# A new order for the first group of an mLSTM and SwiGLU kernel

## The chip, the cores and the metric

The kernel runs on one core of a Trainium2 chip. The metric is the time of one execution on the device in microseconds (us). Five engines work side by side, each through its own instructions in a fixed order: TensorE (PE, matrix products), VectorE (DVE), ScalarE (ACT), GpSimd (POOL) and SyncE (SP, which here only issues DMAs). An engine that waits holds up everything that stands behind the waiting instruction.

## The reference

First comes an mLSTM cell with q, k, v and an output gate of shape (4, 8, 768, 40): batch, heads, steps, width. The cell's rows, heads side by side, are then the 3072 x 320 input of a SwiGLU block.

```python
for t in range(S):                       # for every batch and head
    m_new  = max(f_gate[t] + m, i_gate[t])
    f_stab = exp(f_gate[t] + m - m_new);  i_stab = exp(i_gate[t] - m_new)
    C = f_stab * C + i_stab * outer(v[t], k[t])
    n = f_stab * n + i_stab * k[t]
    y[t] = sigmoid(o_gate[t]) * (C @ q[t]) / max(abs(n @ q[t]), 1)
g = x @ w_gate                           # x: y as (3072, 320); w_gate, w_val: (320, 1536)
out = (g * sigmoid(g) * (x @ w_val)) @ w_out      # w_out: (1536, 320)
```

## The kernel before

**Groups.** The 768 steps are cut into six groups of 128 steps (`L`), and a group of all four batches gives 512 rows for the SwiGLU block. The recurrence is computed in chunks: inside a chunk as masked and weighted scores, across chunks through a state `C`. The 32 pairs of batch and head are worked on in two halves, `P` = 0 and 1. Group 0 has its own code (the functions named `first_...`), since it has no state before it; the other groups go through `turn`, `scores`, `weigh`, `add`, `next_state`, `attend`, `gather`, `gate`, `divide` and `seam`.

**Group 0**, in front of everything: `first_mask`, `first_inputs` and `first_maxima` build the exponents of the weights in PSUM, `first_exp` exponentiates them into `h_sb` (which is free until the hidden blocks need it), `first_turn` transposes k and q on PE and copies them out, `first_scores` multiplies k and q on PE, and DVE multiplies the weights by it (line 480). `first_own(u)` multiplies the weights by v for batch u, `first_x(u)` divides (lines 492 to 495), `first_gate(P)` multiplies by the output gate, whose sigmoid `sig(P)` is taken on ACT, `first_seam(P, engs)` transposes the result into `xT`, with the engines of its three copies given as letters (A is ACT, V is DVE), and `first_state(P, eng)` makes the state for the next group. `late_sums` and `late_maxima` are the running sums and maxima of the gates for groups 1 to 5. `burn(n)` issues n matmuls on a tile of zeros whose result nobody reads.

**Hidden blocks.** `hidden(g, m)` makes block m of twelve of the hidden layer of group g: ten fp32 matmuls (line 593), a SiLU on ACT (598) and a product on DVE (599). Then `project` or `project_all` multiplies by `w_out` (609, 616). In group 0, further work is hung between the hidden blocks by hand in a table `slots`: after block m, the calls of `slots[m]` are issued.

**Weights.** They arrive as fp32 in pieces (`piece_load`), by SP's queue. `convert(j)` rounds block j in three steps: `scale` on ACT (lines 184 and 186, from `raw` to `top` and `low`), `join` on DVE (194, 195, to `both`) and `rounded` (202) on POOL, or on DVE where V is given: block 0 and, by `on_vector`, blocks 9, 10 and 11. `top`, `low` and `both` have one buffer each, so block j+1 follows block j. In the loop over group 0, `convert(m + 2)` is issued behind the matmuls of block m and ahead of its SiLU. Pieces 0 and 1 hold one block each, pieces 2 to 6 two blocks each (piece 6: blocks 10 and 11), pieces 7 to 9 hold `w_out`. The tile `raw` has two buffers, so the load of piece 4 waits until `scale(0)` has read piece 0, and so on.

**Weights of the scores in group 1.** `late_maxima` stores the maxima to memory (`M_dram`, line 285), `weights_load` reads them back spread over partitions into `w_sb` (404), `weights_sub` subtracts on DVE (408), `weights_mask` masks on POOL (413, two instructions for each P), `weights_exp` exponentiates on ACT (417), and `weigh_values` multiplies v by the last column on POOL (320).

**What sets the order.** The kernel is written under a manual schedule: on each engine the instructions stand in the order in which the functions are called. PSUM is eight banks in two rotations of four: "cell" (transposes, scores, adds, burns) and "gen" (first_own, hidden blocks, projections). A bank is taken again only when the tile four before it in the same rotation has been read.

Of the kernel before, what the change touches and what calls it, by code (L numbers as in the profile page):

```python
# [24 lines left out]
def kernel(  # L25
# [47 lines left out]
    def flat(t):  # L73
        return t.rearrange("p c t -> p (c t)")

    def bank(name, tag="cell"):
        return psum.tile([128, 512], F32, name=name, tag=tag)

    def half(i):
        return slice(i * SUB, (i + 1) * SUB)  # L80

    def heads(P):
        return slice(P * UH, (P + 1) * UH)

    k_sb = const.tile([128, BH, DP], F32)
    q_sb = const.tile([128, BH, DP], F32)
# [5 lines left out]
    qT = const.tile([128, PP, L], F32)  # L92
# [22 lines left out]
    def copy(eng, dst, src):  # L115
        if eng is nc.scalar:
            nc.scalar.copy(dst, src)
        else:
            eng.tensor_copy(dst, src)
# [59 lines left out]
    def scale(j):  # L179
        if j in blocks:  # L180
            lo, hi, dst = blocks[j]
            a, d = hi.shape[1], hi.shape[2]
            top = conv.tile([128, NKC * 128], F32, name="top", bufs=1).rearrange("p (a d) -> p a d", a=a)
            nc.scalar.mul(top, hi.bitcast(F32), 2.0 ** -112)  # L184
            low = conv.tile([128, NKC * 128], I32, name="low", bufs=1).rearrange("p (a d) -> p a d", a=a)
            nc.scalar.mul(low, lo, 2.0 ** -29)
            blocks[j] = (low, top.bitcast(U32), dst)

    def join(j):
        if j in blocks:  # L190
            lo, top, dst = blocks[j]
            a = dst.shape[1]
            both = conv.tile([128, NKC * 128], U32, name="both", bufs=1).rearrange("p (a d) -> p a d", a=a)
            nc.vector.tensor_scalar(both, top, scalar1=3, scalar2=None, op0=ALU.logical_shift_left)  # L194
            nc.vector.scalar_tensor_tensor(both, in0=top, scalar=0x80000000, in1=both, op0=ALU.bitwise_and,  # L195
                                           op1=ALU.bitwise_or)
            blocks[j] = (lo, both, dst)

    def rounded(j, eng=None):
        if j in blocks:  # L200
            lo, both, dst = blocks.pop(j)
            (eng or nc.gpsimd).tensor_tensor(dst.bitcast(I32), both.bitcast(I32), lo, op=ALU.add)  # L202

    def convert(j, eng=None):
        scale(j)
        join(j)
        rounded(j, eng)
# [64 lines left out]
    def late_sums():  # L272
        nc.vector.tensor_tensor_scan(flat(f_sb), flat(keep1), flat(f_sb), 0.0, op0=ALU.mult, op1=ALU.add)
        nc.gpsimd.memset(step1, 0.0)
        nc.vector.tensor_sub(i_sb, i_sb, f_sb)
        nc.vector.tensor_copy(step1[:, 0:1, 0:1], f0[0:BH, end].unsqueeze(1))
        nc.vector.tensor_copy(step1[:, 1:, 0:1], f_sb[:, 0:NL - 1, last])
# [57 lines left out]
    def state(s):  # L335
        return C_ring[s % 3]
# [82 lines left out]
    def sig(P):  # L419
        nc.scalar.activation(o_sb[:, heads(P)], o_sb[:, heads(P)], AF.Sigmoid)  # L420


    def burn(n):
        t = bank("burn")
        for _ in range(n):
            nc.tensor.matmul(t, lhsT=junk[:, 0:128], rhs=junk, start=True, stop=True)
# [4 lines left out]
    A, V, G = nc.scalar, nc.vector, nc.gpsimd  # L431
# [29 lines left out]
    def first_turn(P, src, dst, engs):  # L461
        for b in range(2):
            tp = bank("tp_kq").rearrange("p (a t) -> p a t", t=L)
            for a in range(UA // 2):
                h = P * UH + b * H + 2 * a
                nc.tensor.transpose(tp[:, a, :], src[:, h:h + 2, :].rearrange("p h d -> p (h d)"), ident)
            a = P * UA + b * UA // 2
            copy(engs[b], dst[:, a:a + UA // 2, :], tp)

    def first_scores(P):  # L470
        for b in range(2):
            sp = [bank("sp").rearrange("p (a t) -> p a t", t=L) for _ in range(2)]
            a0 = P * UA + b * UA // 2
            for a in range(UA // 2):
                for two in range(2):
                    nc.tensor.matmul(sp[two][:, a, :], lhsT=kT[half(two), a0 + a, :], rhs=qT[half(two), a0 + a, :],
                                     start=True, stop=True)
            W = W0[:, 2 * a0:2 * a0 + H].rearrange("p (a two) t -> p two a t", two=2)
            for two in range(2):
                nc.vector.tensor_tensor(W[:, two], sp[two], W[:, two], op=ALU.mult)  # L480
# [3 lines left out]
    def first_own(u):  # L484
        first_y[u] = bank("first_y", "gen")[:, 0:H * D1].rearrange("p (h d) -> p h d", d=D1)
        for h in range(H):
            nc.tensor.matmul(first_y[u][:, h, :], lhsT=W0[:, u * H + h, :], rhs=v_sb[:, u * H + h, :], start=True, stop=True)

    def first_x(u):
        y = first_y.pop(u)  # L490
        den = work.tile([128, UH, 1], F32, name="den")[:, 0:H]
        nc.vector.tensor_scalar(den, y[:, :, D:], scalar1=1.0, scalar2=None, op0=ALU.max)
        nc.vector.scalar_tensor_tensor(den, in0=y[:, :, D:], scalar=-1.0, in1=den, op0=ALU.mult, op1=ALU.max)
        nc.vector.reciprocal(den, den)
        nc.vector.tensor_tensor(x_sb[:, u, 0:DM].rearrange("p (h d) -> p h d", d=D), y[:, :, 0:D],
                                den.to_broadcast([128, H, D]), op=ALU.mult)

    def first_gate(P):
        for u in (2 * P, 2 * P + 1):
            x = x_sb[:, u, 0:DM].rearrange("p (h d) -> p h d", d=D)  # L500
            nc.vector.tensor_tensor(x, x, o_sb[:, u * H:(u + 1) * H], op=ALU.mult)
        nc.gpsimd.tensor_copy(x_sb[:, 2 * P:2 * P + 2, DM:], x_sb[:, 2 * P:2 * P + 2, 0:HP])

    def first_state(P, eng):
        ps = small("add")
        for a in range(UA):
            for two in range(2):
                h = P * UH + 2 * a + two
                nc.tensor.matmul(ps[half(two), a, :], lhsT=k_sb[:, h, :], rhs=vw_sb[:, h, :], start=True, stop=True)
        copy(eng, state(2)[:, P * UA:(P + 1) * UA], ps)  # L510

    def first_seam(P, engs):
        for c, eng in zip(range(0, NKC, 2), engs):
            cs = range(c, min(c + 2, NKC))
            tp = bank("tp_x")[:, 0:len(cs) * 2 * L].rearrange("p (c u s) -> p c u s", u=2, s=L)
            for w in cs:
                for b in range(2):
                    nc.tensor.transpose(tp[:, w - c, b, :], x_sb[:, 2 * P + b, ds(PAIRS[w][0] * HP, 2 * HP)], ident)
            copy(eng, xT(0)[:, c:c + len(cs), 2 * P * L:(2 * P + 2) * L].rearrange("p c (u s) -> p c u s", u=2), tp)
# [10 lines left out]
    first_exp(1)  # L530
    first_values(0)
    first_scores(0)
    late_sums()
    first_own(0)
    first_turn(1, k_sb, kT, (A, A))
    first_own(1)
    first_turn(1, q_sb, qT, (A, V))
    sig(0)
    first_values(1)
    first_x(0)  # L540
    first_x(1)
    first_scores(1)
    first_own(2)
    first_own(3)
    first_x(2)
    first_gate(0)
    first_x(3)
    sig(1)
    first_seam(0, (A, A, A))
    first_gate(1)  # L550
    first_state(0, A)
    first_seam(1, (V, A, V))
    first_state(1, A)
    burn(6)
    convert(0, V)
    convert(1)


    pair = early.tile([BH, PP], F32)
# [94 lines left out]
    def load_all(dst, a, n):  # L654
        for P in range(2):
            load(dst, a, n, P)

    run = lambda f, *a: (lambda: f(*a))
# [3 lines left out]
    slots = {  # L662
        0: [run(load_all, k_sb, k, 1), run(load_all, q_sb, q, 1), run(piece_load, 5), run(late_maxima)],
        1: [run(decay_rows)],
        2: [run(late_turns), run(weights_load, 1)],
        3: [run(decay)],
        4: [run(piece_load, 6), run(load_all, v_sb, v, 1)],
        5: [run(turn, 0, (A, A), (A, V))],
        6: [run(turn, 1, (A, A), (A, V)), run(piece_load, 7)],
        7: [run(weights_sub, 1, 0), run(weights_mask, 0)],  # L670
        8: [run(weights_sub, 1, 1), run(weights_mask, 1), run(weights_exp, 0), run(weights_exp, 1),
            run(weigh_values, G, 0), run(weigh_values, G, 1), run(piece_load, 8)],
        9: [run(do_scores), run(do_weigh, 0), run(load_all, o_sb, o_gate, 1)],
        10: [run(do_weigh, 1), run(do_add), run(do_state, 2, 0), run(do_state, 2, 1), run(piece_load, 9)],
        11: [run(do_attend, 1, 0), run(do_gather, 1, 0, False)],
# [1 line left out]
    piece_load(4)  # L677
    for m in range(NFC):
        hidden(0, m, [run(convert, m + 2, V if m + 2 in on_vector else None)])
        for f in slots[m]:  # L680
            f()
    after = {
        0: [run(do_attend, 1, 1), run(convert, 14), run(sig, 0), run(sig, 1), run(do_gate, 0)],
# [21 lines left out]
    for g in range(1, NG):  # L705
        n, f = g + 1, g + 2
        slots = {m: [] for m in range(NFC)}
# [63 lines left out]
```

## Time and profile before

| what | value |
|---|---|
| runs | 584.78, 584.83, 587.49 us; median 584.83 |
| profiled execution | 583.13 us, of which the span of instructions is 581.3 us |
| mean granted TensorE clock | 0.994 |
| busy in the span | PE 567.3 us, DVE 209.2, ACT 150.9, POOL 99.6 |
| first matmul of hidden block 0 | at 37.62 us |
| first matmul of group 1 (its block 0) | at 138.03 us |

The profile is of one execution. Its lines of the timeline give start in us, duration in us, engine, source line, operation, output and inputs with shapes, and the number of instructions merged into one line; the bracket gives the idle time of the engine before it and who ended it. PEclk is the TensorE clock granted, 1.00 being full speed. SPq lines are DMA issues; their duration is how long SP took to issue, not to move the data.

### The profile page before, as it was taken

What the parts mean: (1) busy time and instruction counts of PE and PEld (TensorE: products, weight loads), DVE (VectorE), ACT (ScalarE), POOL (GpSimd) and SP (SyncE); (2) the same over time, 40 slices, a digit from 0 to 9 for tenths busy, and PEclk for the clock granted to TensorE, in tenths of its full rate; (3) what the DMA queues carried; (4) which work ended last, traced back from release to release, by engine and by line L of the source; (5) the groups of instructions that cost most, each with busy time, mean ns of one, the idle gap of its engine ahead of it and who ended that gap; (6) DMA issues with size and microseconds to landing.
All of it is one profiled execution on the core that took longest, in us unless ns stands there. A gap on an engine that the chain in (4) does not pass through costs nothing.

```text
span 581.3 us, 12164 instructions
## 1 busy us (share of the span) xinstructions
PE 567.3 (98%) x5404; PEld 329.7 (57%) x5405; DVE 209.2 (36%) x379; ACT 150.9 (26%) x236; POOL 99.6 (17%) x101
## 2 busy tenths in 40 slices
PE   8889988999999999999999999999999999999997
PEld 4854534666555576555566555567555557544475
DVE  5846475880335520334620233640223640011100
ACT  4356555434401115210114311024301110011100
POOL 2122325445001132002132001232001110000000
PEclk9989999999999999999999999999999999999999
DMA  9999896395223711304340304360000000000000
GB/s 124 185 209 154 178 201 153 119 159 106 41 29 43 126 28 36 45 2 70 76 78 24 58 1 47 64 113 23 12 2 2 2 1 24 23 1 0 1 23 23
DMA packets 129915, 37.85 MB, mean 65 GB/s; under 512 B 120424, under 2 KB 125032, under 8 KB 129864
## 3 DMA queue, kind: packets, MB, share of 16 engines
q1 hardware_dynamic: 129636, 36.85, 36.7%
q8 instruction: 42, 0.69, 0.5%
q10 hardware_dynamic: 228, 0.23, 0.2%
q14 instruction: 9, 0.07, 0.0%
HBM read 33.06 MB, written 4.01 MB: 64 GB/s over the span
## 4 chain that ended last, share of the span: by engine, by line
PE 81%; ACT 2%; DVE 1%; DMA 0%; issue 0%; ACTq 0%; DVEq 0%
PE gv_ps L593 45%; PE o_ps L609 22%; PE o_ps L616 4%; PE inter L350 2%; PE intra L355 2%; PE add L331 2%; PE sp L310 1%; PE tp_kq L295 1%; PE tp_x L396 1%; ACT w_sb L417 0%; DMA out_dram<-z_sb 0%; ACT o_sb L420 0%; ACT L598 0%; ACT L420 0%; ACT L417 0%
## 5 line engine op out<-in xcount | busy, mean ns | idle before, releaser
L593 PE MATMUL gv_ps<-xT,wgv_sb 64*128 64x512 f32 x1440 | 323.4, 597 | 5.1 <-DVE wgv_sb L202 5.1
L593 PEld LDWEIGHTS gv_ps<-xT,wgv_sb 64*128 64x128 f32 x1440 | 138.2, 188 | 161.9 <-issue 152.3
L599 DVE TENSOR_TENSOR h_sb<-sg,gv_ps 128x512 f32<-128x512 f32 x72 | 49.4, 687 | 304.2 <-ACT sg L598 287.3
L609 PE MATMUL o_ps<-wo_sb,h_sb 128*128 128x320 f32 x480 | 130.5, 433 | 0.0
L598 ACT ACTIVATE sg<-gv_ps 128x512 f32<-128x512 f32 x72 | 43.0, 598 | 269.2 <-PE gv_ps L593 269.2
L609 PEld LDWEIGHTS o_ps<-wo_sb,h_sb 128*128 128x128 f32 x480 | 90.8, 190 | 38.2 <-issue 0.8
L340 POOL TENSOR_TENSOR C<-C,dec 128x328 f32<-128x328 f32 x20 | 14.5, 737 | 165.0 <-DVE C L342 165.0
L603 ACT COPY z_sb<-o_ps 128x320 f32<-128x320 f32 x24 | 10.2, 426 | 114.4 <-PE o_ps L609 103.0
L413 POOL TENSOR_SCALAR_AFFINE_SELECT w_sb<-w_sb 64x1024 f32<-64x1024 f32 x20 | 26.3, 1314 | 29.6 <-DVE w_sb L408 28.7
L616 PE MATMUL o_ps<-wo_sb,h_sb 128*128 128x320 f32 x96 | 26.9, 437 | 0.0
L376 POOL TENSOR_TENSOR o_sb<-o_sb,y_sb 128x640 f32<-128x640 f32 x10 | 14.2, 1429 | 48.4 <-DVE y_sb L367 48.4
L616 PEld LDWEIGHTS o_ps<-wo_sb,h_sb 128*128 128x128 f32 x96 | 17.9, 190 | 7.2
L367 DVE TENSOR_TENSOR y_sb<-y_sb,intra 64x328 f32<-64x328 f32 x40 | 19.7, 493 | 0.9
L320 POOL TENSOR_TENSOR vw_sb<-v_sb,w_sb 128x656 f32<-128x656 f32 x10 | 12.8, 1306 | 29.4 <-issue 29.3
L202 POOL TENSOR_TENSOR wgv_sb<-both,low 128x640 int32<-128x640 int32 x8 | 12.3, 1540 | 30.3 <-DVE both L195 30.3
L195 DVE SCALAR_TENSOR_TENSOR both<-top,both 128x640 uint32<-128x640 uint32 x18 | 15.7, 870 | 0.6
L194 DVE TENSOR_SCALAR both<-top 128x640 uint32<-128x640 uint32 x18 | 10.2, 565 | 12.9 <-ACT top L184 10.4
L350 PEld LDWEIGHTS inter<-C,qT 64*64 64x64 f32 x640 | 10.2, 134 | 7.3 <-issue 6.1
L202 POOL TENSOR_TENSOR wo_sb<-both,low 128x640 int32<-128x640 int32 x6 | 10.2, 1704 | 18.3 <-DVE both L195 12.9
L184 ACT ACTIVATE top<-raw 128x640 f32<-128x640 f32 x14 | 11.1, 795 | 8.2 <-DVE both L195 5.8
L408 DVE TENSOR_TENSOR w_sb<-g_T,w_sb 128x1024 f32<-128x1024 f32 x10 | 13.2, 1350 | 0.0
L342 DVE TENSOR_TENSOR C<-C,add 128x328 f32<-128x328 f32 x20 | 9.8, 492 | 8.7 <-POOL C L340 8.7
(120 smaller groups left out, 379.2 us busy)
## 6 DMA issues: line engine op xcount, KB each, us to landing
w_sb<-M_dram SPq DMA_DIRECT2D x10, 512.0 KB, 6.7
k_sb<-in_k_dram SPq DMA_DIRECT2D x12, 320.0 KB, 7.0
q_sb<-in_q_dram SPq DMA_DIRECT2D x12, 320.0 KB, 4.1
v_sb<-in_v_dram SPq DMA_DIRECT2D x12, 320.0 KB, 5.5
o_sb<-in_o_gate_dram SPq DMA_DIRECT2D x12, 320.0 KB, 6.8
raw<-in_moe_w_out_dram SPq DMA_DIRECT2D x3, 1280.0 KB, 7.3
out_dram<-z_sb SPq DMA_DIRECT2D x24, 160.0 KB, 1.8
raw<-in_moe_w_gate_dram SPq DMA_DIRECT2D x3, 640.0 KB, 9.3
```

Source lines behind the costliest of these rows:

```text
L195: nc.vector.scalar_tensor_tensor(both, in0=top, scalar=0x80000000, in1=both, op0=ALU.bitwise_and, op1=ALU.bitwise_or)
L202: (eng or nc.gpsimd).tensor_tensor(dst.bitcast(I32), both.bitcast(I32), lo, op=ALU.add)
L340: nc.gpsimd.tensor_tensor(state(s + 1)[:, a], state(s)[:, a], dec[:, s - 2, a].unsqueeze(2).to_broadcast([128, UA, D1]), op=ALU.mult)
L350: nc.tensor.matmul(inter[two][half(i), a, :], lhsT=qT[half(two), P * UA + a, half(i)], rhs=state(2 * n + i)[half(two), P * UA + a, :], sta ...
L367: nc.vector.tensor_tensor(t, t, intra[i][half(c)], op=ALU.add)
L376: eng.tensor_tensor(o, o, y[:, :, 0:D], op=ALU.mult)
L413: nc.gpsimd.affine_select(w, w, compare_op=ALU.is_ge, fill=NEG, base=0, pattern=[[0, UH], [1, SUB]], channel_multiplier=-1)
L593: nc.tensor.matmul(ps[i], lhsT=wgv_sb[half(i), PAIRS[kc][i], ts(m, 128)], rhs=x[half(i), kc, :], start=(kc == 0), stop=(kc == NKC - 1))
L598: nc.scalar.activation(sg, ps[0], AF.Silu)
L599: nc.vector.tensor_tensor(hid(g, m), sg, ps[1], op=ALU.mult)
L609: nc.tensor.matmul(p, lhsT=hid(g, m)[:, ts(u, L)], rhs=wo_sb[:, m, :], start=(m == 0), stop=(m == NFC - 1))
L616: nc.tensor.matmul(ps[u], lhsT=hid(g, m)[:, ts(u, L)], rhs=wo_sb[:, m, :], start=(m == 0), stop=(m == NFC - 1))
```

## The change

The calls of group 0 are put in a new order, which is a new order on every engine. The transposes of q for P = 1 go ahead of `first_own(1)`. `first_x(0)` follows the transposes of k. Both sigmoids come together. `burn(6)` at the end becomes `burn(3)`, `burn(5)` and `burn(4)` at three places. `first_gate` of P = 0 goes ahead of `first_x(2)`. The third copy of each `first_seam` goes to DVE and the first two to ACT. `scale(0)` and `join(0)` are issued between the two seams and `rounded(0)` behind the second. Both `first_state` follow both seams. `late_sums` moves from the middle to behind `convert(1)`.

In the table for group 0, slot 5 becomes empty: the two `turn` calls move from slots 5 and 6 to 6 and 7, both `weights_sub` and both `weights_mask` stand together in slot 7, and slot 8 keeps the exponentials, `weigh_values` and the load of piece 8. SP's DMAs stay in the same order. Nothing is computed differently.

```diff
     first_scores(0)
-    late_sums()
     first_own(0)
     first_turn(1, k_sb, kT, (A, A))
+    first_x(0)
+    first_turn(1, q_sb, qT, (A, V))
     first_own(1)
-    first_turn(1, q_sb, qT, (A, V))
-    sig(0)
     first_values(1)
-    first_x(0)
     first_x(1)
     first_scores(1)
+    sig(0)
+    sig(1)
+    burn(3)
     first_own(2)
     first_own(3)
+    first_gate(0)
     first_x(2)
-    first_gate(0)
+    first_seam(0, (A, A, V))
+    burn(5)
     first_x(3)
-    sig(1)
-    first_seam(0, (A, A, A))
     first_gate(1)
+    scale(0)
+    join(0)
+    first_seam(1, (A, A, V))
+    rounded(0, V)
     first_state(0, A)
-    first_seam(1, (V, A, V))
     first_state(1, A)
-    burn(6)
-    convert(0, V)
+    burn(4)
     convert(1)
+    late_sums()
...
-        5: [run(turn, 0, (A, A), (A, V))],
-        6: [run(turn, 1, (A, A), (A, V)), run(piece_load, 7)],
-        7: [run(weights_sub, 1, 0), run(weights_mask, 0)],
-        8: [run(weights_sub, 1, 1), run(weights_mask, 1), run(weights_exp, 0), run(weights_exp, 1),
-            run(weigh_values, G, 0), run(weigh_values, G, 1), run(piece_load, 8)],
+        6: [run(turn, 0, (A, A), (A, V)), run(piece_load, 7)],
+        7: [run(turn, 1, (A, A), (A, V)), run(weights_sub, 1, 0), run(weights_sub, 1, 1), run(weights_mask, 0),
+            run(weights_mask, 1)],
+        8: [run(weights_exp, 0), run(weights_exp, 1), run(weigh_values, G, 0), run(weigh_values, G, 1),
+            run(piece_load, 8)],
```

More of the change, by code (lines that the diff above doesn't have):

```diff
@@ L679 @@
         hidden(0, m, [run(convert, m + 2, V if m + 2 in on_vector else None)])
-        for f in slots[m]:
+        for f in slots.get(m, ()):
             f()
```

## The prediction

> **What bounds the kernel now.** The page gives TensorE (PE) 567.3 us of a span of 581.3. A gain is therefore either idle PE time, or PE time at a low clock, ahead of 100 us; behind that the matmuls stand end to end. The page's DMA row (40 slices of 14.5 us) and the waits of PE:
>
> ```profile
> DMA  9999896395223711304340304360000000000000
> PE gv_ps L593 <- DVE wgv_sb L202: 5.1, 4, 2.2
> ```
>
> The loads fill every slice up to 72 us, and PE's longest waits are for weights (`wgv_sb`) that VectorE (DVE) has rounded. PE's timeline shows where; from here on h0 to h11 are the twelve hidden blocks of the first group:
>
> ```profile
> 78.66 4.56 PE L593 MATMUL gv_ps<-xT,wgv_sb 64*128 64x512 f32 x20 [0.19 <-DVE wgv_sb L202]
> 84.61 4.56 PE L593 MATMUL gv_ps<-xT,wgv_sb 64*128 64x512 f32 x18 [1.39 <-DVE wgv_sb L202]
> 89.09 2.10 PE L310 MATMUL sp<-qT,kT 64*64 64x64 f32 x128
> 91.12 1.12 PE L593 MATMUL gv_ps<-xT,wgv_sb 64*128 64x512 f32 x2
> 93.60 4.55 PE L593 MATMUL gv_ps<-xT,wgv_sb 64*128 64x512 f32 x18 [1.35 <-DVE wgv_sb L202]
> ```
>
> These are h8, h9, the scores of group 1, and h10, whose first matmul runs alone before the rest waits. DVE shows what they wait for:
>
> ```profile
> 80.68 1.22 DVE L194 TENSOR_SCALAR both<-top 128x640 uint32<-128x640 uint32 x1 [0.35 <-ACT top L184]
> 81.93 1.63 DVE L195 SCALAR_TENSOR_TENSOR both<-top,both 128x640 uint32<-128x640 uint32 x1
> 83.73 0.83 DVE L202 CUSTOM_DVE_ANT_0 wgv_sb<-both,low 128x1280 uint16<-128x1280 uint16 x1 [0.17 <-DVE both L195]
> 92.72 0.83 DVE L202 CUSTOM_DVE_ANT_0 wgv_sb<-both,low 128x1280 uint16<-128x1280 uint16 x1 [0.17 <-DVE both L195]
> ```
>
> Blocks 9, 10 and 11 are rounded on DVE. Block 10's rounding ends at 84.56 and lets **h9** go at 84.61; block 11's ends at 93.55 and lets **h10** go: the DVE rounding is taken for a write to the whole tile, so each block waits for the rounding of the next. What held those two back stands on ScalarE (ACT) and GpSimd (POOL):
>
> ```profile
> 79.86 0.79 ACT L184 ACTIVATE top<-raw 128x640 f32<-128x640 f32 x1 [1.61 <-DMA raw<-in_moe_w_val_dram]
> 88.72 1.06 ACT L417 ACTIVATE w_sb<-w_sb 128x1024 f32<-128x1024 f32 x1 [3.34 <-POOL w_sb L413]
> 89.68 0.80 ACT L184 ACTIVATE top<-raw 128x640 f32<-128x640 f32 x1
> 80.41 2.49 POOL L413 TENSOR_SCALAR_AFFINE_SELECT w_sb<-w_sb 64x1024 f32<-64x1024 f32 x2 [7.57 <-DVE w_sb L408]
> 86.36 2.33 POOL L413 TENSOR_SCALAR_AFFINE_SELECT w_sb<-w_sb 64x1024 f32<-64x1024 f32 x2 [3.46 <-DVE w_sb L408]
> ```
>
> Block 10 starts when piece 6 has landed (79.86). Its join (L194, L195) then runs beside the mask of pair half 0 and takes 1.22 and 1.63, against 0.49 and 0.82 elsewhere. Block 11 (89.68) stands on ACT behind exp(1), which waits for mask(1). Why piece 6 lands at 79.86 is on SP's queue and in the list of DMA issues:
>
> ```profile
> 56.56 0.55 SPq L285 DMA_DIRECT2D M_dram<-M_sb  x1
> 64.92 2.12 SPq L404 DMA_DIRECT2D w_sb<-M_dram  x2
> 67.13 2.70 SPq L159 DMA_DIRECT2D raw<-in_moe_w_gate_dram  x1
> 69.88 1.28 SPq L159 DMA_DIRECT2D raw<-in_moe_w_val_dram  x1
> M_dram<-M_sb SPq DMA_DIRECT2D x1, 80.0 KB, 8.4
> ```
>
> 80 KB take 8.4 us, since they queue behind the loads issued before; SP stands still until 64.92 for them, and piece 6 is issued after. So **79.86 is a date of the DMA queue**, not of any engine. Last, two stretches of the windows view (us, then PE, PEld, DVE, ACT, POOL busy, PEclk, DMA share, GB/s):
>
> ```profile
> 27.70:31.10 3.40, 3.40 (x30) 2.90 (x29) 2.06 (x7) 1.45 (x3) 0.59 (x2) 0.51 1.09 211
> 38.00:41.30 3.30, 3.30 (x10) 1.39 (x8) 1.51 (x4) 1.74 (x3) 1.54 (x1) 0.50 1.07 215
> ```
>
> PE ran at half clock for 3.4 us twice, both in the part that the change rewrites.
>
> [...] two stretches of 3.4 us, the second after 2.17 us of idle PE (35.45 to 37.62). The first followed no long gap, only 128x41 matmuls[...]. [...]
>
> **The change part by part.**
>
> *Front.* In the old order DVE did late_sums (2.5 us) and both first_x of P=0 (4 instructions, 1.1 us each) before the last score products, which began at 22.98. In the new one the transposes of q (P=1) go ahead of first_own(1): that load has landed by about 17.8 (issued at 10.25; the v load behind it landed at 20.0; 2.2 us each), so first_own(1) ends at about 20.4 and the scores start at 20.4 as before (20.50). first_x(1) then ends at 21.6, and the products run 21.6 to 24.1: 1.4 earlier. PE: scores to 22.4, burn(3) 0.7 (0.25 each: 1.47 for six in the row of 33.98), first_own(2) and (3) 3.5, to 26.6 (before 27.85). first_seam(0) at full clock takes 1.3 (2.49 before), burn(5) 1.2. DVE: gate(0) 24.1 to 25.0, x(2), a seam copy at 28.0, x(3) and gate(1) to 30.3. first_seam(1) 30.0 to 31.7, both states 2.1, burn(4) 1.0: h0 at about **34.7** (37.62 before). Weights: scale(0) runs behind the first two seam copies on ACT (28.4 to 29.9; piece 0 was issued at 20.9 and takes 5.3), join(0) to 31.6, rounding to 33.1: hidden. With the 1.7 us of half clock at 38.0 to 41.3 gone (if the 12 burns keep the clock up; 6 before), h0 ends 4.6 earlier. late_sums now sits on DVE behind join(1), about 36.5 to 39, ahead of block 2's join and h0's product; POOL's memset likewise ahead of rounding 2. The maxima are ready at about 43, and their store stands in SP's queue until 56.56 anyway: free.
>
> *DMAs.* SP's order is the same. Piece 4 can be issued at 30 instead of 35.92, k of group 1 at 33.8 instead of 37.27, but [...] the dates 56.56, 64.92 and 79.86 stay. Value: 0.
>
> *Slots 5 to 8.* turn moves from slots 5 and 6 to 6 and 7. turn(1), 0.98 us of transposes, now covers the rounding of block 9 between h7 and h8 (a bubble of 1.1 before). h8 then ends at about 34.7 + 9x4.35 (h4 and h5: 8.69) + 3.2 (small transposes 0.73, decay 0.47, turns 0.98 and 0.99) = 77.1 instead of 83.0. Both subs (1.22 each) run on DVE from about 74.2 to 76.6, the four masks (1.17 each) on POOL to about 80.1, just clear of join(10) at 80.5.
>
> *From piece 6 on.* join(10) 0.49+0.82 instead of 1.22+1.63: h9 at 83.0, **1.6 earlier**. The lead of 5.8 that h8 had is waited away there. ACT: scale(10) to 81.15, silu(8), table 1.28, both exps to 85.1, scale(11) to 86.5; join(11) to 88.0 even beside weigh_values on POOL; rounding to 88.9. PE: h9 4.5, scores 2.0: h10 at 89.4, no wait. Before it had lost 93.60 - 91.12 = **2.5** there. Sum 4.1. Later work keeps its own spacing.
>
> *Against it.* Between h8's end (the lone first matmul of h9 included: about 78.1) and 83.0 PE idles 4.9 us, far more than the 2.17 that cost the clock before. [...] I take **1.5**.
>
> Net -2.6 against the profiled execution's 583.13: 580.5. The median of the runs, 584.83, is 1.7 above that execution, as much as one whole 3.41 us stretch at half clock costs. If it is one in the waits before h10, it goes with them (580.5); if it is anything else it stays (582.2). The trace can't tell; I take between: **581.4**.
>
> **Rivals.**
> 1. *The clock holds through the wait*: -4.1, so 579.0 to 580.7. Against: 2.17 us were enough. Chance 0.12.
> 2. *The DMA date moves up*, because pieces 4 and k are issued 3.5 to 6 earlier; dips in the rate of the 160-byte loads (45 to 60 us: 157 GB/s against 210) leave room for 1 to 2. About 579.5. Against: the queue never ran dry. Chance 0.15.
> 3. *The masks still meet join(10)*: the margin is 0.4 us. Up to 1.5 of the 1.6 goes: -1.0, so 582 to 584. Chance 0.18.
> 4. *Slower*: late_sums is late, the maxima miss their place in SP's queue, and SP holds w_sb and piece 6 behind them. One for one from 56.6; slower by over 0.5% from about 62. For it: five instructions were moved 20 us back. Against: a margin of 13 us. About 588. Chance 0.10.
> The main case has 0.45.
>
> **How the numbers follow.** 0.5% is 2.9 us, about what a measurement of this kernel can tell from no change. The main case spans 580 to 583.5 with somewhat over half below 581.9; with rivals 1 and 2: faster 0.56. The rest of it and rival 3: same 0.34. Rival 4: slower 0.10. The range 579.0 to 584.0 leaves out rival 4 and the tails of 1 to 3.
>
> **What would show it.** h0 at about 34.7 with PEclk 1.00 from 27 on; h8 ending near 77; piece 6 still waited for until 79 to 80; L194 at 0.49 there; PE idle for about 5 us before h9; a half-clock stretch just behind 83; no wait ahead of h10, near 91. I am wrong if piece 6 lands before 78, if h0 starts after 39, or if the wait ahead of h10 is still there.

## The result and the profile after

The changed kernel takes 583.56 us (median of 20 runs, 582.18 to 585.58), the kernel before 584.79 (20 runs, 583.92 to 587.49). The ratio is 0.9966, 95% interval 0.9953 to 0.9979. That is a third of a per cent: a gain, but below the 0.5% that the prediction set as its bound for "faster". The profiled execution of after took 583.69 us, close to its median; that of before took 583.13, below every one of those 20 runs. Set side by side, the two profiles, both with a mean granted clock of 0.994, show no gain at all: the first matmul of group 1 starts at 138.60 after and at 138.03 before.

On the page of after, the row of the granted clock (40 slices of 14.5 us):

```profile
PEclk9999988999999999999999999999999999999999
```

The low clock, which before stood in the third slice (29 to 44 us), now stands in the sixth and seventh (73 to 102 us). PE's timeline after (start, duration, engine, line, operation, shapes, count, and in brackets the idle time before and who ended it; the hidden matmuls are line 597 now, and the ten of a block give 20 records):

```profile
34.35 13.28 PE L597 MATMUL gv_ps<-xT,wgv_sb 64*128 64x512 f32 x60
49.49 4.73 PE L597 MATMUL gv_ps<-xT,wgv_sb 64*128 64x512 f32 x20 [1.14 <-POOL wgv_sb L202]
...
73.93 5.37 PE L597 MATMUL gv_ps<-xT,wgv_sb 64*128 64x512 f32 x22
84.03 7.63 PE L597 MATMUL gv_ps<-xT,wgv_sb 64*128 64x512 f32 x18 [4.74 <-DVE wgv_sb L202]
...
93.61 4.56 PE L597 MATMUL gv_ps<-xT,wgv_sb 64*128 64x512 f32 x20
...
100.27 0.28 PE L331 MATMUL add<-vw_sb,k_sb 64*64 64x41 f32 x2 [1.02 <-DVE w_sb L317]
```

The x60 are h0 to h2; the 20 matmuls at 49.49 are h3; the x22 are h8 and the two records of h9's lone first matmul; then h9, h10 (right behind the scores of group 1) and the second add. h0 starts 3.3 us earlier than before and h8 ends 3.9 earlier. Then PE idles for 4.74 us ahead of h9, which gets away only 0.58 us earlier than in the profile before (84.03 against 84.61) and takes 7.63 us instead of 4.56. The wait ahead of h10 is gone, but h10 starts where it did (93.61; before 93.60). What held h9, on ACT, DVE and POOL:

```profile
79.21 0.79 ACT L184 ACTIVATE top<-raw 128x640 f32<-128x640 f32 x1 [4.02 <-DMA raw<-in_moe_w_val_dram]
80.03 1.28 DVE L194 TENSOR_SCALAR both<-top 128x640 uint32<-128x640 uint32 x1 [2.48 <-ACT top L184]
81.35 1.63 DVE L195 SCALAR_TENSOR_TENSOR both<-top,both 128x640 uint32<-128x640 uint32 x1
75.20 2.35 DVE L408 TENSOR_TENSOR w_sb<-g_T,w_sb 128x1024 f32<-128x1024 f32 x2
76.49 5.82 POOL L413 TENSOR_SCALAR_AFFINE_SELECT w_sb<-w_sb 64x1024 f32<-64x1024 f32 x4 [7.82 <-DVE w_sb L408]
```

Piece 6 lands at 79.2. join(10) then runs at 1.28 and 1.63 us, as slowly as before, because the four masks (76.49 to 82.31) still stand on POOL (e4, without them, has 0.49 and 0.83). The view of that tile gives the durations of the four (ns, least, median, most):

```profile
L413 POOL TENSOR_SCALAR_AFFINE_SELECT w_sb<-w_sb x4: 1138/1220/2062, 76.5 to 81.0; 64x1024 f32<-64x1024 f32 x4
```

The long one is the first, beside the second sub (76.3 to 77.5). The windows view of the stretches behind h9's start (us, then PE, PEld, DVE, ACT, POOL busy, PEclk, DMA share, GB/s):

```profile
83.70:87.00 3.30, 2.97 (x8) 1.43 (x10) 2.66 (x4) 3.28 (x4) 2.70 (x2) 0.50 0.58 200
87.00:90.50 3.50, 3.50 (x10) 1.34 (x9) 0.61 (x1) 0.12 (x1) 0.00 (x0) 0.54 0.93 318
```

PE has half its clock for about 6.8 us, two stretches end to end: h9 pays 3.07 us for it (7.63 less 4.56).

SP's queue, whose dates the prediction held to be fixed (the duration is that of issuing):

```profile
56.32 0.55 SPq L285 DMA_DIRECT2D M_dram<-M_sb  x1
64.87 2.51 SPq L404 DMA_DIRECT2D w_sb<-M_dram  x2
...
69.70 0.61 SPq L159 DMA_DIRECT2D raw<-in_moe_w_val_dram  x1
```

56.56 became 56.32, 64.92 became 64.87, and piece 6's second half is issued at 69.70 (69.88): the dates did not move with the front.

### The profile page after: what moved, and what is told of

Read it like the earlier page. It is cut to its first block, busy times and chain, and to the rows that moved or that the text cites. A ratio compares the mean times of both kernels' runs of the same rounds, so it can differ in the third digit from the quotient of the medians.

```text
span 581.9 us, 12175 instructions
## 1 busy us (share of the span) xinstructions
PE 567.7 (98%) x5411; PEld 332.4 (57%) x5411; DVE 210.9 (36%) x379; ACT 150.9 (26%) x236; POOL 101.7 (17%) x101
## 4 chain that ended last, share of the span: by engine, by line
PE 85%; ACT 2%; DMA 2%; DVE 1%; issue 0%; POOL 0%; SPq 0%; ACTq 0%; DVEq 0%; POOLq 0%
PE gv_ps L597 50%; PE o_ps L613 22%; PE o_ps L620 4%; PE inter L350 2%; PE sp L310 2%; PE intra L355 2%; DMA raw<-in_moe_w_val_dram 2%; PE add L331 2%; PE tp_kq L295 1%; PE tp_x L396 1%; DVE both L195 0%; ACT w_sb L417 0%; DMA out_dram<-z_sb 0%; DVE both L194 0%; ACT sg L602 0%
## 5 line engine op out<-in xcount | busy, mean ns | idle before, releaser
L597 PEld LDWEIGHTS gv_ps<-xT,wgv_sb 64*128 64x128 f32 x1440 | 141.4, 189 | 159.7 <-issue 149.8
L340 POOL TENSOR_TENSOR C<-C,dec 128x328 f32<-128x328 f32 x20 | 14.5, 735 | 166.6 <-DVE C L342 166.6
L320 POOL TENSOR_TENSOR vw_sb<-v_sb,w_sb 128x656 f32<-128x656 f32 x10 | 13.0, 1320 | 30.7 <-issue 29.4
L331 PEld LDWEIGHTS add<-vw_sb,k_sb 64*64 64x64 f32 x640 | 10.1, 135 | 5.3 <-issue 4.2
```

The source lines that it names most:

```text
L331: nc.tensor.matmul(ps[i][half(two), a, :], lhsT=k_sb[half(i), h, :], rhs=vw_sb[half(i), h, :], start=True, stop=True)
L340: nc.gpsimd.tensor_tensor(state(s + 1)[:, a], state(s)[:, a], dec[:, s - 2, a].unsqueeze(2).to_broadcast([128, UA, D1]), op=ALU.mult)
L597: nc.tensor.matmul(ps[i], lhsT=wgv_sb[half(i), PAIRS[kc][i], ts(m, 128)], rhs=x[half(i), kc, :], start=(kc == 0), stop=(kc == NKC - 1))
```

## The experiments

In the table every line is one kernel. Dates are from its profiled execution, medians and ratios from the timed runs of each kernel against the kernel before on the same chip (whose median was 584.6 to 584.8 each time). From the start of group 1 to the end the profiles differ by less than 0.6 us (before 581.3 - 138.03 = 443.3, after 443.3, the extremes 442.9 and 443.4), so the start of group 1 says what an execution will take. The column "half clock" counts stretches of about 3.4 us at a clock of 0.50 behind 20 us in the profile. The column "clock" is the median, over the timed runs, of the mean granted clock of each run.

| kernel | h0 | h9 | h10 | group 1 | half clock | median us | clock | ratio [95%] |
|---|---|---|---|---|---|---|---|---|
| before, profile of the prediction | 37.62 | 84.61 | 93.60 | 138.03 | 2 | 584.79 | 0.991 | 1 |
| before, another execution (e6) | 39.61 | 86.21 | 95.20 | 139.63 | 3 | 584.72 (one run) | 0.991 | |
| after | 34.35 | 84.03 | 93.61 | 138.60 | 2 | 583.56 | 0.994 | 0.9966 [0.9953, 0.9979] |
| after, another execution (e7) | 34.41 | 83.57 | 91.62 | 138.32 | 2 | 583.50 (one run) | 0.994 | |
| e1 new front, old slots | 35.92 | 82.78 | 91.76 | 137.90 | 2 | 582.17 | 0.996 | 0.9949 [0.9931, 0.9967] |
| e2 old front, new slots | 39.59 | 87.73 | 95.94 | 140.96 | 4 | 586.41 | 0.987 | 1.0015 [1.0003, 1.0028] |
| e3 burns in the wait | 35.93 | 86.77 | 93.29 | 138.56 | 2 | 581.84 | 0.997 | 0.9937 [0.9916, 0.9958] |
| e4 no masks | 35.92 | 82.62 | 89.13 | 134.20 | 1 | 579.52 | 0.996 | 0.9902 [0.9878, 0.9925] |
| e5 piece 6 ahead in SP's queue | 34.15 | 79.53 | 86.05 | 132.42 | 0 | 579.44 | 0.9965 | 0.9908 [0.9879, 0.9936] |
| e8 as e5, SP's order kept | 35.93 | 82.78 | 89.29 | 137.30 | 2 | 582.16 | 0.994 | 0.9954 [0.9938, 0.9971] |
| e9 as e5, old front | 40.18 | 85.72 | 92.24 | 138.78 | 4 | 583.99 | 0.988 | 0.9987 [0.9977, 0.9997] |
| e10 block 10 rounded on POOL | 34.28 | about 78.4 | 89.16 | 133.59 | 0 | 579.96 | 0.9965 | 0.9929 [0.9910, 0.9948] |
| e11 all blocks rounded on POOL | 34.33 | about 80.0 | 86.37 | 135.28 | 3 | 577.18 | 0.996 | 0.9883 [0.9862, 0.9905] |
| e12 before, all blocks on POOL | 39.60 | about 83.8 | 90.12 | 140.05 | 5 | 584.94 | 0.985 | 0.9995 [0.9982, 1.0009] |

(h9 and h10: where their second records begin if the lone first matmul ran ahead. "About": the blocks stand in one line of the timeline there, and the date comes from sharing that line's time evenly between them. The clock of the kernel before is that of its 76 runs beside the experiments.)

The clock column gives an estimate of what low clock costs: in a time T at a mean clock c, PE loses at most (1 - c) T, since a stretch at half clock does half the work (h9 of e2, with one stretch of 3.4 us in it, takes 6.25 us instead of 4.56). That is 5.3 us in the kernel before and 3.5 in the changed one. The difference, 1.8 us, is more than the whole gain of 1.2: apart from the clock the changed kernel is no faster.

The theory at the start: piece 6's date sets h9, so the front's lead is lost and the slots bring the gain, which masks and clock then take back. The rival: the front brings the gain and the slots nothing.

### e1 and e2: the two halves of the change

e1 keeps the old table of slots under the new front:

```diff
+        5: [run(turn, 0, (A, A), (A, V))],
+        6: [run(turn, 1, (A, A), (A, V)), run(piece_load, 7)],
+        7: [run(weights_sub, 1, 0), run(weights_mask, 0)],
+        8: [run(weights_sub, 1, 1), run(weights_mask, 1), run(weights_exp, 0), ...
```

> The new order of group 0, with the old slots table. Theory (the date of piece 6 in the DMA queue swallows the front's lead): h0 starts near 34.4, h8 ends near 78, piece 6 still lands at 79 to 80; join(10) meets mask(0) as before (1.2 and 1.6 us), so h9 starts at about 84; PE idles over 4 us there and h9 runs at half clock; h10 near 93.6, as in both kernels. Time equal to the changed kernel's and to the kernel before's profiled one, 583 to 584, within 0.3%. Rival (the front is what gains): 2 to 4 us faster than the kernel before.

e2 is the reverse, the old front with the new table.

> The old order of group 0, with the new slots table. Theory: h0 at 37.6, h8 ends near 81 to 82, so PE idles only about 2 us before h9 (at about 84, since the masks meet join(10) still) and the clock holds; h10 then follows the scores at 90.5 instead of 93.6: 2 to 3 us faster than the kernel before, and faster than the changed kernel by 1 to 3 us. Rival (the slots do nothing without the early front): equal to the kernel before within 0.2%.

Measured: e1 582.17, 0.9949; e2 586.41, 1.0015. The new front alone is faster than the kernel before by half a per cent, the new slots alone are slower by 0.15%, and the two together (0.9966) lie where the two add up. The rival came true in both: I had expected e1 to equal the changed kernel, and it is 2.6 us faster than the kernel before; my expectation of e2, two to three us faster, was wrong in sign. DVE's and PE's timelines of e2 say why:

```profile
80.63 2.35 DVE L408 TENSOR_TENSOR w_sb<-g_T,w_sb 128x1024 f32<-128x1024 f32 x2
82.90 1.43 DVE L194 TENSOR_SCALAR both<-top 128x640 uint32<-128x640 uint32 x1
...
87.73 6.25 PE L593 MATMUL gv_ps<-xT,wgv_sb 64*128 64x512 f32 x18 [3.01 <-DVE wgv_sb L202]
```

With the late front both subs come at 80.63, the moment at which `top` of block 10 is being made (80.49 on ACT), and hold up join(10) by themselves; the masks then lie beside the whole of it (1.43 and, behind the line shown, 1.63, and 1.51 for the rounding). h9 starts 1.5 us later than in e6 and runs at half clock. By the clock column e2 loses 7.6 us to low clock, 2.4 more than the kernel before, so its loss of 1.7 in time is one of clock as well.

In e1, ACT waits for piece 6 until 78.72 and only the first mask pair meets join(10), and slows its second step alone (the first takes 0.49):

```profile
80.09 1.64 DVE L195 SCALAR_TENSOR_TENSOR both<-top,both 128x640 uint32<-128x640 uint32 x1
```

h9 goes at 82.78, 1.25 us earlier than in the changed kernel, at full clock; in this execution a half-clock stretch falls on h10 instead (91.76, 6.25 us). The idle time of over 4 us ahead of h9 did not come: it is 1.45 us, because h8 and the lone matmul end at 81.32 there (79.30 in the changed kernel), with h0 1.6 us later by a half-clock stretch in the front. Between e1 and the changed kernel the intervals overlap, though all eleven runs of e1 lie below the median of the changed kernel: that the new slots cost 1.4 us under the new front is likely and not shown for certain; that they bring nothing is.

### e3 and e4: the clock and the masks at h9

e3 fills the wait ahead of h9 with matmuls that nobody reads:

```diff
-            run(piece_load, 8)],
+            run(piece_load, 8), run(burn, 22)],
```

> The changed kernel with 22 more idle matmuls between h8 and h9, where PE waits (about 4.9 us of them). Theory (the wait costs the clock: h9 took 7.6 us instead of 4.6): no half clock from 83 to 90, h9 takes 4.6, h10 starts at about 90.6 instead of 93.6: 3 us faster than the changed kernel's profile, about 580.5. Rival (something else holds h10, the rounding of block 11): h10 stays at 93.6 and the time at 583.5.

e4 leaves the four masks of group 1 out, so its time is that of a kernel that does not mask these weights.

```diff
-        7: [run(turn, 1, (A, A), (A, V)), run(weights_sub, 1, 0), run(weights_sub, 1, 1), run(weights_mask, 0),
-            run(weights_mask, 1)],
+        7: [run(turn, 1, (A, A), (A, V)), run(weights_sub, 1, 0), run(weights_sub, 1, 1)],
```

> The changed kernel without the four masks of group 1 (so the weights of later steps are not set to zero there). Theory (the masks still meet join(10)): L194 and L195 of block 10 take 0.49 and 0.82, h9 starts at about 82.5 instead of 84.0; h9 still at half clock, so h10 about 1.5 us earlier, near 92. Rival (join(10) is slow for another reason, such as the DMA): 1.3 and 1.6 as in the changed kernel, h9 at 84.

PE in e3, then in e4:

```profile
81.92 4.92 PE L426 MATMUL burn<-junk 128*128 128x512 bf16 x21
86.77 4.56 PE L597 MATMUL gv_ps<-xT,wgv_sb 64*128 64x512 f32 x20
```

```profile
82.62 4.55 PE L597 MATMUL gv_ps<-xT,wgv_sb 64*128 64x512 f32 x18 [1.75 <-DVE wgv_sb L202]
```

The burns (22 issued, 21 in the trace) stand from 81.92 to 86.84. With PE kept busy h9 runs at full speed (4.56 us). Beside the other kernels that fits: behind waits of 4.74 (after), 4.23 (e7) and 3.01 us (e2) h9 ran at half clock, behind 0.41 to 1.90 us (e1, e4, e5, e6, e8, e9) it did not. It is no fixed threshold: 3.14 us ahead of h10 in e10 cost nothing, 2.17 us ahead of h0 in the kernel before were followed by a stretch, and so were 1.35 us ahead of h10 in e1 and 1.14 ahead of h3 in e3. The dates of the theory did not come in this profile (h10 at 93.29, where 90.6 was expected): the burns end at 86.8, later than h9 went in the changed kernel, and a stretch fell on h3. It is the slowest of the nine runs. In the medians the net is 1.7 us (583.56 less 581.84), which is what the clock accounts for: 3.5 us lost in the changed kernel, 1.7 in e3. Without masks join(10) takes 0.49 and 0.83, and h9 goes 1.4 us earlier, at full clock where I had expected half: masks in the way of join(10) and the clock lost behind the longer wait together cost the changed kernel 4.0 us (583.56 less 579.52). The two are not independent, since the wait ahead of h9 is only 1.75 us in e4; and 1.6 of the 3.0 by which it is shorter come from h0, which a stretch in the front made late in this profile (35.92).

### e5, e8 and e9: the date of piece 6

e5 issues piece 6 ahead of the load of the weights on SP, and moves subs and masks behind join(10), exponentials behind the scores:

```diff
-        2: [run(late_turns), run(weights_load, 1)],
+        2: [run(late_turns)],
-        4: [run(piece_load, 6), run(load_all, v_sb, v, 1)],
+        4: [run(piece_load, 6), run(weights_load, 1), run(load_all, v_sb, v, 1)],
-        7: [run(turn, 1, (A, A), (A, V)), run(weights_sub, 1, 0), run(weights_sub, 1, 1), ...
+        7: [run(turn, 1, (A, A), (A, V))],
+        8: [run(weights_sub, 1, 0), run(weights_sub, 1, 1), run(weights_mask, 0), run(weights_mask, 1),
+        9: [run(do_scores), run(weights_exp, 0), run(weights_exp, 1), run(weigh_values, G, 0), run(weigh_values, G, 1),
```

> The changed kernel with the load of piece 6 issued ahead of the reload of w_sb on SP (so that it does not stand behind the landing of M_dram), and the subs and masks of group 1 in slot 8, the exponentials and weigh_values in slot 9. Theory (the date of piece 6 and the masks beside join(10) set h9): piece 6 lands at about 71, join(10) runs at 0.49 and 0.82, PE goes from h8 to h9 with about 1 us of wait, the clock holds, h10 starts at 86 to 88 instead of 91.8 to 93.6: 4 to 7 us faster than the changed kernel, about 577 to 579. Rival (w_sb, now later by 6 us, becomes the bound through exp, weigh and add): h11 no earlier than in the changed kernel, 582 to 584.

e8 has e5's slots with SP's order unchanged, e9 has e5's slots and SP order under the old front.

> The same slots as the kernel with piece 6 first, but with SP's DMAs in the old order: piece 6 lands at 79 to 80. Theory: join(10) is clear of the masks, so h9 starts at about 82.7; the masks now meet join(11), and h10 starts at about 90 to 91: 1 to 3 us faster than the changed kernel, and 3 to 4 slower than with piece 6 first. Rival (the order of the loads adds nothing, the place of the masks is all): equal to the kernel with piece 6 first.

> The front of the kernel before, with the slots and the SP order of e5_dma_order (piece 6 issued ahead of weights_load(1)). This asks what the new front is worth once the transfer of piece 6 is not in the way. Theory A (the front's lead was only swallowed by the date of piece 6): h0 starts near 39.6 instead of 34.2, h9 at about 84 to 85 instead of 79.5, and the time is 4 to 5 us above e5_dma_order, near 583.5 to 584.5. Theory B (the front is worth nothing in itself): the time equals that of e5_dma_order, 579.4, within 1 us.

SP and PE of e5, and PE of e9:

```profile
61.03 0.59 SPq L159 DMA_DIRECT2D raw<-in_moe_w_gate_dram  x1
79.53 4.55 PE L597 MATMUL gv_ps<-xT,wgv_sb 64*128 64x512 f32 x18 [0.42 <-DVE wgv_sb L202]
```

```profile
85.72 4.56 PE L593 MATMUL gv_ps<-xT,wgv_sb 64*128 64x512 f32 x18 [0.41 <-DVE wgv_sb L202]
```

Piece 6, issued 6.4 us earlier, is in place long before it is needed, PE waits 0.42 us for h9 where it waited 4.74, and no half-clock stretch follows. e5 against e8 is the SP order alone: 579.44 against 582.16, 2.7 us. e5 against e9 is the front alone with piece 6 out of the way: 579.44 against 583.99, **4.5 us**, of the 6.0 us by which h0 starts earlier in these two profiles. That is theory A as written for e9. What the front gives is mostly clock: by the clock column e9 loses 7.0 us and e5 2.0, a difference of 5.0 (an estimate). Whether the order or the twelve burns in new places keep the clock up, no run separates. e8 against the changed kernel (582.16 against 583.56, intervals overlapping) is what e5's slots do while piece 6 still lands at 79.5: the masks meet join(11) there instead of join(10), and h9 goes at 82.78.

### e6 and e7: the same two kernels again

Both kernels as they are, one execution each, to see how far one profile stands for the kernel.

> The kernel before, profiled once more on this chip. Theory (its first profiled execution was an early one: 583.13 against a median of 584.8): h0 starts later than 37.6, at about 39.5, so that h8 ends near 85 and PE, not the date of piece 6, sets h9. Rival (h0 at 37.6 again, and the time differs behind h10).

> The changed kernel, profiled once more on this chip. Theory: h0 at 34.4 to 36, the masks meet join(10) again (1.3 or more, and 1.6), h9 at 84 to 87; what differs from the first profile is where the half-clock stretches fall. Rival: the masks are clear of join(10) in most executions, and the first profile was an exception.

PE and the windows view of e6, the kernel before:

```profile
39.61 14.84 PE L593 MATMUL gv_ps<-xT,wgv_sb 64*128 64x512 f32 x60 [2.18 <-DVE wgv_sb L202]
86.21 4.55 PE L593 MATMUL gv_ps<-xT,wgv_sb 64*128 64x512 f32 x18 [1.00 <-DVE wgv_sb L202]
```

```profile
26.60:30.00 3.40, 3.40 (x20) 3.40 (x19) 2.07 (x8) 0.00 (x0) 0.29 (x1) 0.54 1.10 213
30.00:33.40 3.40, 3.40 (x39) 3.07 (x39) 1.59 (x5) 1.45 (x3) 0.30 (x1) 0.50 1.07 208
```

Here the front of the kernel before loses two stretches of clock ahead of h0 instead of one, and h0 starts 2 us later. One more stretch follows in h0 to h2, as in the profile of the prediction. `scale(10)` at 80.13 waits for no DMA, h8 ends at 85.21, and h9 waits 1.00 us behind it. Block 10 is joined by 84.41, but its rounding on DVE waits for h8 on PE, and h9 then waits for the rounding:

```profile
85.33 0.83 DVE L202 CUSTOM_DVE_ANT_0 wgv_sb<-both,low 128x1280 uint16<-128x1280 uint16 x1 [0.93 <-PE gv_ps L593]
```

So in this execution, whose time of 584.72 is that of the median, **PE and not piece 6 sets h9**. The front's lead then does count. e2 and e12, which share the old front, have the same h0 (39.59 and 39.60) and the same stretches up to there. In e7 the masks meet join(10) again: its second step takes 1.64 us, the rounding 1.51, and h9 goes at 83.57.

### e10, e11 and e12: does h9 need piece 6?

One line is changed, under the new kernel for e10 (9, 11) and e11 (empty), under the old one for e12 (empty):

```diff
-    on_vector = (9, 10, 11)
+    on_vector = (9, 11)
```

> The changed kernel with one number changed: block 10 is rounded on GpSimd instead of VectorE (on_vector = (9, 11)). Theory A (h9 does not need piece 6 at all; it waits for block 10 only because the VectorE rounding is taken for a write to the whole tile): h9 starts right behind h8, at about 78.4, TensorE has no 4.7 us of idle there, the clock holds, and h10 starts at about 87 to 88, set by block 11; some 5 us below the changed kernel, near 578. Theory B (h9 waits for something else that comes with piece 6): h9 still starts at about 84 and the time stays at 583.5.

> The changed kernel with all blocks of the first group rounded on GpSimd (on_vector empty). Theory A (as for e10_block10_pool, for h8, h9 and h10 alike): h9 at about 78.3, h10 near 85, h11 near 93 to 94, no wait of TensorE for a later block; 7 to 8 us below the changed kernel, 575.5 to 577. Theory B (GpSimd becomes the bound: the masks, the weighing of the values and three more roundings of 1.5 us stand in one queue there): a wait of several us ahead of the addition to the hidden product or ahead of h11 takes the place of the one removed, near 580.

> The kernel before with all blocks of the first group rounded on GpSimd (on_vector empty). Theory A (the wait ahead of h10 in the kernel before, 2.5 us in its profile and up to 3.5 us in another execution, comes from block 11's rounding on VectorE alone): h9 follows h8, h10 starts near 90, some 5 us below the kernel before, near 580. Theory B (with the late front TensorE sets the dates itself): no difference, 584.5.

PE of e10, of e11 and of e12:

```profile
73.87 9.07 PE L597 MATMUL gv_ps<-xT,wgv_sb 64*128 64x512 f32 x40
89.16 4.56 PE L597 MATMUL gv_ps<-xT,wgv_sb 64*128 64x512 f32 x18 [3.14 <-DVE wgv_sb L202]
```

```profile
75.61 8.81 PE L597 MATMUL gv_ps<-xT,wgv_sb 64*128 64x512 f32 x40
```

```profile
90.12 4.56 PE L593 MATMUL gv_ps<-xT,wgv_sb 64*128 64x512 f32 x20
98.94 0.41 PE L331 MATMUL add<-vw_sb,k_sb 64*64 64x41 f32 x2 [1.41 <-DVE w_sb L317]
```

In e10 ACT waits for piece 6 until 78.95 as ever, the masks still slow join(10), and yet h8 and h9 run as one block of 40 from 73.87 to 82.94. **h9 never needed block 10**; the wait came with the rounding on DVE alone. What in that rounding holds PE is not shown (on POOL it is another instruction as well, 128x640 int32 instead of 128x1280 uint16). The prediction took it for a write to the whole tile. That cannot be quite so, since the first matmul of h9 runs ahead of it (in the changed kernel it ends at 79.30, and the rounding runs from 83.15 to 83.98). Why the next matmul waits was not shown.

The wait then sits ahead of h10, for block 11, which is still rounded on DVE: 3.14 us. The gain over the changed kernel is 3.6 us, where some 5 were expected. e11 takes that one away too and is the fastest kernel of the study, 577.18 us, 1.2% below the kernel before and 6.4 us below the changed one (7 to 8 were expected); its profiled execution (579.95 us) was the slowest of its five runs, with half clock in h3 and again about h11. Theory B's wait did show in part (1.50 us ahead of the second add, 1.02 in the changed kernel) but small.

e12 is neither theory as I wrote it. h10 starts at 90.12 as theory A had it, 5.1 us earlier than in e6 (where 2.5 us are lost ahead of h10, as in the first profile), and the time is that of the kernel before all the same. The adds wait 1.11 and 1.41 us, the waits are followed by two half-clock stretches (98.4 to 105.2, h11 takes 6.52), and h11 ends at 107.93, against 107.52 in e6. The old slots put exp(1) behind the second mask, and that behind a rounding on POOL (exp(1) runs at 90.09, e11 has it at 84.27): what was saved ahead of h10 turned into a wait, and a low clock, behind it. Which of front and slots makes e11 7.8 us faster than e12 is not told apart; by the clock column 6.5 of them are clock (2.3 us lost against 8.8).

A kernel with e5's SP order and e11's roundings was not run.

## Why the prediction was right, and where its steps failed

The time lay in the range, 2.2 us above the number: a gain within 0.5%, which had a chance of 0.34, where faster by more than that, with 0.56, was the likeliest. That the range held is in part luck. The gain is about a third of the 3.4 us that were forecast, and it came from the front, which the sum had put at nothing, while the 4.1 us of the slots were lost again. Against the profiled execution, the sum said -2.6; the two profiles differ by +0.56. Three terms make up the 3.1 between them.

- **The mask term (1.6 predicted, 0.58 measured), the step that failed first.** It was priced as four masks of 1.17 us from 75.4 on, "just clear of join(10)". The first mask took 2.06 us, beside the second sub, against 1.14 for the shortest of the four, and the four took 5.82 us, from 76.49 to 82.31. The prediction reckoned with a mask beside a join (1.22 and 1.63 in its trace), but not with a sub beside a mask. The masks also started 1.1 us later than planned, by the wait ahead of h3 below. And the margin of 0.4 us would have gone even at the planned times (masks to 80.1), for piece 6 came early and join(10) started at 80.03. The 0.58 is piece 6 landing 0.65 us earlier. This is rival 3, given 0.18.
- **The clock term (1.5 taken; 3.07 measured).** That the clock would fall behind the idle PE came true; with the wait filled (e3) or short (e4) it did not fall there. The 1.5 was the author's estimate, a little under the 1.7 us that a stretch of 3.41 us at 0.50 costs (27.74 to 31.15 in the profile before), and so assumed one stretch; the profile has two (83.4 to 90.2). In e7 it was one, 1.5 us (h9 takes 6.09 instead of 4.56), the value that was taken; a second stretch came 14 us later. So two executions of one kernel paid 3.07 and 1.5 us there. The prediction took 2.17 us of idle PE to be enough for a low clock. How long PE has to idle for it was not shown: 2.17 us (before, ahead of h0) and 3.01 us (e2, ahead of h9) were followed by a stretch, 3.14 us (e10, ahead of h10) were not.
- **The wait ahead of the second add (not in the sum; 0.55).** It rose from 0.47 to 1.02; its cause stays open.

1.0 + 1.6 + 0.55 = 3.1. The right term: the 2.5 us ahead of h10 came as forecast, there is no wait there.

**The front** went nearly as worked out: h0 at 34.35 (34.7 predicted), no half clock in it in this profile. In four of the eight other profiles with the new front (e1, e3, e4, e8) it kept one stretch at 27.3 to 30.7 and h0 came at 35.9: "if the burns keep the clock up" holds in some executions only. h8 with the lone matmul ended at 79.30 instead of 78.1, since h3 waits 1.14 us, which the prediction did not see. Its cause is a chain, here on ACT and POOL of after:

```profile
44.89 0.74 ACT L284 ACTIVATE keep<-keep 32x640 f32<-32x640 f32 x1 [2.14 <-DVE keep L283]
47.90 1.54 POOL L202 TENSOR_TENSOR wgv_sb<-both,low 128x640 int32<-128x640 int32 x1 [5.43 <-DVE both L195]
```

Block 3's scale (45.53) stands on ACT behind the exponential of the late maxima (44.89), so its rounding ends 15.1 us behind the start of h0 (49.44 less 34.35). Before it was 14.7 (52.31 less 37.62), and h0 to h2 took 14.84, half clock in them: the lost clock hid the chain. At full clock they take 13.28, and PE stands before it. late_sums in its new place has the 0.4 us of it: its product on DVE took 1.97 us (0.81 before), beside block 1's rounding on POOL, 2.58 us (1.54 before). The wait itself cost nothing in the end, for h9 waits anyway; it did move the masks.

**The dates of SP's queue** held (rival 2 falls). The reading that the store queues behind the loads has its numbers in the profile before: the load issued at 55.84 landed after 8.9 us, at 64.7, and the store issued behind it at 56.56 after 8.4, at 65.0. The store of the maxima missed nothing (rival 4 falls; 56.32 against 56.56). The clock did not hold (rival 1 falls; rival 3 came true in kind).

**What the sum stood on** was the second failure. It was made against one execution, 583.13, and the 1.7 us up to the median were left open between the waits ahead of h10 and "anything else". e6 shows them in the front: one more half-clock stretch, h0 2 us later. The profile of the prediction was a rare draw: of the 76 runs of the kernel before beside the experiments, three have its clock of 0.994 (583.1 to 583.3 us) and 45 have 0.991 (583.9 to 585.1). That moves more than an offset. In the typical execution PE sets h9 and the front's lead is worth 2.2 us there (86.21 to 84.03), not the 0 that followed from "the lead is waited away". The account of after against e6 closes: 5.9 us of lead where h8 ends, less 3.7 of added wait, less 3.1 of clock, plus 2.5 ahead of h10, less 0.55 at the add: 1.0, and group 1 starts at 138.60 against 139.63. e1 and e2 say the same from outside: the gain of 0.34% is the front's, by the clock that it keeps, and the slots, which the sum credited with 4.1 us, bring none of it.

## What to carry to other kernels

Before a lead is credited or written off, look for what the waiting engine needs in truth: here a false dependence on the rounding of the next block held PE for 4.7 us, and under the new front one changed line (`on_vector`) was worth more than the whole reordering. A piece of work that is moved is to be checked against everything that then runs beside it on the other engines, its own neighbours included, and the margin taken at the slowed durations (here 2.06 us for a mask beside a sub against 1.14, and 1.43 and 1.63 for a join beside masks against 0.49 and 0.83). One profile is one draw: where clock stretches fall differently from one execution to the next, take a second profile of the kernel before, since which engine sets a date can differ between executions. And read the granted clock of the timed runs beside their times: here, by the estimate above, it accounts for the whole gain.

## What the runs showed of the hardware

- With the four masks on POOL beside it, DVE's join took 1.43 and 1.63 us (1.64 in e8) instead of 0.49 and 0.83, and its custom rounding 1.51 instead of 0.83 (e2, e5, e8), while the four masks took 6.76 us instead of the 5.82 of after. The masks pay as well as the join.
- Half clock fell in the middle of busy PE: from 26.6 to 33.4 in e6 the windows have PE busy all of the time with matmuls of 128x41 and transposes, at 0.54 and 0.50. In e9 it lasted from about 24.4 to 34.6.
- The spread between executions of one kernel goes with the granted clock. In e5 the runs at 0.999 took 577.5 and 577.7 us, those at 0.996 and 0.997 took 579.2 and 579.7, one at 0.994 took 581.1 and one at 0.991 took 582.6. In the kernel before, the 45 runs at 0.991 took 583.9 to 585.1 and the 14 at 0.987 took 586.6 to 587.0.
